# Half of a weight-gradient product moved one step earlier, and the first group's products in another order

## The chip, the cores and the metric

The kernel runs on one core of a Trainium2 chip. A core has a matrix engine (TensorE, PE in the profile, with its weight loads as PEld), a vector engine (VectorE, DVE), a scalar engine (ScalarE, ACT), GpSimd (POOL) and SyncE (SP), which here only issues DMA transfers. Each engine takes its instructions in the order in which they stand in its own queue and waits for the others by semaphores. The metric is the device time of one execution in microseconds, the median of several. Matmul results land in PSUM, a small memory of eight banks, and must be copied out of it (evacuated) by ACT or DVE before the bank can be used again.

## What is computed

It is the backward pass (and the output) of a layer that mixes a spectral filter with a gated feed-forward network, all in bf16, with 2048 rows of 576 and an inner width of 4608:

```python
def _A_ref(x, w_r, w_i):                       # spectral filter
    X = rfft2(x) * (w_r + 1j * w_i)
    return irfft2(X, s=(S, D))

def _B_ref(x, w_gate, w_up, w_down):           # feed-forward
    return (_gelu(x @ w_gate) * (x @ w_up)) @ w_down

g = _sigmoid((x * gate_w).sum(-1, keepdims=True))
out = g * _A_ref(...) + (1 - g) * _B_ref(...)
# results: out, and the gradients for x, w_r, w_i, w_gate, w_up, w_down, gate_w
```

## The kernel before

The kernel has two phases. The first, some 950 us long, goes over the 4608 inner columns in 18 groups (`g` = 0 to 17, `NG`) of 256 columns. Each group is four steps (`m` = 0 to 3, called the first to the fourth step here), and a step takes 512 of the 2048 rows. The code counts steps through as `pr` = 4 g + m. The second phase, from about 980 us to the end, multiplies the stored activations with the weights (L1205) and is not touched.

A step does three kinds of work.

- **The step's own forward part.** `H_mm` (L403) issues the products `z` (grad_out times w_down, L413 and L418) and `xy` (x times w_gate and w_up, L422 and L429, in two halves: `xy_full(0)` and `xy_full(1)`). ACT evacuates them: `H_da` (L441, four instructions) for `z`; `H_act` (L448 the square `q`, L450 `xb`, L451 `hu`) for each half of `xy`. DVE then does `H_ew1` (L456 to L460). `sigs`, that is `H_ew2` (L476 to L491), is issued at the end of the step: sigmoids on ACT and seven or eight elementwise instructions on DVE, which make the tiles `A` and `dH`.
- **Weight gradients of the group before.** `W_units` (L514) makes, for one group, four units `d` (`u_dwd`: d_w_down, L535, 16 matmuls of 288 columns each, in two halves of 8) and four units `w` (`u_dw`: d_w_gate and d_w_up together, L553, 16 matmuls of 512 columns, in quarters of 4) and a `tail` (L567, 32 short matmuls). Each unit ends with an evacuation out of PSUM (L504, on ACT as a rule) and a DMA to the output. Two PSUM buffers (`wps`) take turns among the units. The list that `W_units` returns says which unit goes to which step of the next group: entries 0 to 3 are the four steps, entry 4 is carried over to the first step of the group after that, and the dictionary names what goes inside a step, between `H_da` and `xy_full(0)` (the `tail` in the third step).
- **A spectral unit now and then.** The FFT is cut into small units (two to sixteen matmuls into a PSUM tile `pf`, an evacuation on ACT, sometimes a few instructions on DVE and a DMA). `want(pr)` says how many have to be done by each step. From the ninth step on (`pr` > 7) one of them is put inside `xy_full(1)`. The others are spread between the quarters and halves of the weight units: the loop at L1085 walks through `jobs` (the carried units, then the step's own), adds up their weights (3.45 for a whole `w`, 2.0 for a whole `d`) and issues the next spectral unit when the sum has come to its share. `pf` and `z` share one PSUM buffer (`pz`, `bufs=1`, L350), so a spectral unit waits until the one before it is evacuated, and so does the next step's `z`. Groups 2 to 5 do the forward transforms (L596, L613), groups 6 to 12 the middle part (L705, L794; its products are DVE work that `side_work` issues right after `H_ew1`, L710 to L766), groups 12 to 16 the inverse (L841 to L875).

In every step the order on PE is thus: `z`, the thin part of `xy`, what goes inside, `xy_full(0)`, `xy_full(1)` with a spectral unit in it, and the jobs with the other spectral units between them. ACT and DVE follow in the same order.

One more thing belongs to the opening: `dB` holds grad_out, which the `d` units need scaled by one minus the gate. `scale_dB(k, cp)` (L979) scales the four row tiles 4k to 4k+3, on ACT (L982) or on DVE (L984). Unit `d` reads row tiles 0 to 7 in its first half and 8 to 15 in its second. Steps `pr` = 4 to 7 are those of group 1, which carry group 0's weight units. In `pr` = 6, `run_late` (L1090) puts two loads of function tables and four sines on ACT's queue in front of the first job's evacuation, and for the rest of that step the evacuations of weight units go to DVE instead of ACT (L1091).

Of the kernel before, what the change touches and what calls it, by code (L numbers as in the profile page):

```python
# [255 lines left out]
def kernel(  # L256
# [246 lines left out]
    def wevac(out, in_):  # L503
        wcopy[0](out, in_)  # L504
# [9 lines left out]
    def W_units(g):  # L514
        fsl = slice(g * FG, (g + 1) * FG)
        kt = kept[g]

        def tl(k, t):
            tile_ = kt[t // 4][min(k, 1)]
            return tile_[:, t % 4, :] if k == 0 else tile_[:, t % 4, k - 1, :]  # L520
        dwd_tiles, wp = {}, {}

        def halves(f, us):
            return [(us, lambda: f(0)), (us, lambda: f(1))]

        def wtile(key):
            if key not in wp:
                wp[key] = pw.tile([P, TPB, FG], F32, tag="wps", name="wps")
            return wp[key]

        def u_dwd(fch, h):
            def f(half):
                wps = wtile(("d", fch, h)).rearrange("p a b -> p (a b)")
                for t in range(8 * half, 8 * half + 8):
                    nc.tensor.matmul(wps[:, :288], lhsT=tl(0, t)[:, fch * P:(fch + 1) * P],  # L535
                                     rhs=dB[:, t, h * 288:(h + 1) * 288], start=(t == 0), stop=(t == T - 1))
                if half == 0:
                    return
                if h == 0:
                    dwd_tiles[fch] = stage.tile([P, D], BF16, tag="dwd", name="dwd")  # L540
                dwd = dwd_tiles[fch]
                wevac(dwd[:, h * 288:(h + 1) * 288], wps[:, :288])
                if h == 1:
                    r0 = g * FG + fch * P
                    wst[0].dma_start(out_6[r0:r0 + P, :], dwd[:])
            return halves(f, 1.0)

        def u_dw(c, cuts=(0, 4, 8, 12, T)):

            def f(t0, t1):  # L550
                wps = wtile(("w", c))
                for t in range(t0, t1):
                    nc.tensor.matmul(wps[:].rearrange("p a b -> p (a b)"), lhsT=xn[:, t, c * P:(c + 1) * P],  # L553
                                     rhs=kt[t // 4][1][:, t % 4].rearrange("p k f -> p (k f)"), start=(t == 0), stop=(t == T - 1))
                if t1 < T:
                    return
                dw = dwtile("dw")
                wevac(dw[:], wps[:])
                for k, ov in enumerate((o4v, o5v)):
                    wst[0].dma_start(ov[:, c, fsl], dw[:, k, :])  # L560
            return [(3.45 * (b - a) / T, lambda a=a, b=b: f(a, b)) for a, b in zip(cuts, cuts[1:])]

        def tail():
            wps = wtile("t")
            for t in range(T):
                for k, r in ((1, LO), (2, HI)):
                    nc.tensor.matmul(wps[r, 0, :], lhsT=xn[:, t, 512:576], rhs=tl(k, t),  # L567
                                     start=(t == 0), stop=(t == T - 1))
            dw = dwtile("dwt")
            wevac(dw[:, 0], wps[:, 0, :])  # L570
            wst[0].dma_start(out_4[512:576, fsl], dw[LO, 0, :])
            wst[0].dma_start(out_5[512:576, fsl], dw[HI, 0, :])
        w = [u_dw(c, (0, 12, T)) if g == 0 and c < 2 else u_dw(c) for c in range(4)]
        d = [u_dwd(fch, h) for fch in range(FCH) for h in range(2)]
        if g == 0:
            return [[w[0][:1], w[1][:1]], [d[0], d[1]], [d[2], d[3], w[2][:2]], [w[2][2:], w[3][:3]], w[3][3:], {1: [w[0][1][1], w[1][1][1]], 2: [tail]}]
        return [[d[0]], [d[1], d[2], d[3]], [w[0]], [w[1], w[2]], w[3], {2: [tail]}]


    side = []  # L580
# [305 lines left out]
    VC, AC = V.tensor_copy, nc.scalar.copy  # L886
# [5 lines left out]
    for c in range(6):  # L892
        w = gwr[0:1, eo(c)] if c < 4 else gwr[0:1, 512:D]
# [92 lines left out]
    for g in range(NG):  # L986
# [3 lines left out]
        for m in range(NPR):  # L990
            pr = g * NPR + m
# [9 lines left out]
            tiles = [ewt(tag, g) for tag in ("xb", "q", "hu")]  # L1001
            state = []
# [3 lines left out]
            if g == 0:  # L1006
                def items(src, dst, t, *cp):
                    return titems(src, dst, 4 * t, (pgtile,) * 3, cp) if t < NPR else [None] * 3
                do1 = items(dB, dOT, 1, VC, VC, VC) if m == 0 else []
                do2 = items(dB, dOT, m + 2, AC, AC, VC)  # L1010
                x1 = items(xn, xT, m + 1, AC if m else VC, VC, VC)
                z, xy_full = H_mm(g, m, ([opening] if m == 0 else []) + rest)
                rest = []
                da = H_da(g, m, z)
                if m == 0:
                    early, mid_, late_ = do1[:2], [do1[2], x1[0]], x1[1:]
                elif m < NPR - 1:
                    early, mid_, late_ = x1[:2], x1[2:], []
                else:
                    early, mid_, late_ = [], [], []  # L1020
                for f in early:
                    f()
                xy = xy_full(0)
                for f in mid_:
                    f()
                if held:
                    held.pop()()
                for part in (1, 0):
                    H_act(0, xy, tiles, part)

                def between():
                    for f in late_:
                        f()
                xy = xy_full(1, between)
                for part in range(2):
                    H_act(1, xy, tiles, part)
                if m == 0:
                    build_R(nc, tb, unit, 4)
                    columns_B(nc, tb, res)
                elif m == 1:  # L1040
                    next(makeB)
                if m < NPR - 1:
                    gate(m + 1)
                else:
                    V.tensor_copy(g32[:], g_bf[:])
                    V.tensor_scalar(gs32[:], g32[:], SD2, None, op0=ALU.mult)
                if m + 2 < NPR:
                    do2[0]()
                    do2[1]()
                    rest = [do2[2]]  # L1050
                state += [*H_ew1(g, tiles, da), da]
                held.append(sigs)
            else:
                z, xy_full = H_mm(g, m)
                da = H_da(g, m, z)
                for f in inside:
                    f()
                if pr == 5:
                    scale_dB(2, AC)
                xy = xy_full(0)  # L1060
                if held:
                    scale_dB(0, AC)
                    held.pop()()
                for part in (1, 0):
                    H_act(0, xy, tiles, part)
                k0 = int(n > 0 and pr > 7 and ready())
                xy = xy_full(1, fft_next if k0 else None)
                for part in range(2):
                    H_act(1, xy, tiles, part)
                if pr == 5:  # L1070
                    scale_dB(3, VC)
                state += [*H_ew1(g, tiles, da), da]
                if pr == 4:
                    scale_dB(1, VC)
                elif pr == 5:
                    build_R(nc, tb, unit, 8)
                    build_R(nc, tb, unit, 12)
                elif pr == 6:
                    next(makeB)
                side_work(4.4)  # L1080
                jobs = carry + hs
                total = sum(w for w, _ in jobs)
                at, k = 0.0, k0
                tables = {6: 0}.get(pr)
                for i, (w, f) in enumerate(jobs):  # L1085
                    if k < n and (at >= total * k / n - 0.45 or len(jobs) - i <= n - k):
                        fft_next()
                        k += 1
                    if i == tables:
                        run_late(tb)  # L1090
                        wcopy[0] = VC  # L1091
                    if pr == NG * NPR - 1 and at == 0.0:
                        sigs()
                    f()
                    at += w
                wcopy[0] = AC
                while k < n:
                    fft_next()
                    k += 1
                flush()  # L1100
                if pr == 6:
                    next(makeB)
                if pr < NG * NPR - 1:
                    sigs()
# [250 lines left out]
```

## Time and profile before

| what | us |
|---|---|
| median of 3 executions | 1408.48 (1408.42 to 1409.05) |
| the profiled execution | 1408.48, its span 1406.7 |
| PE busy in the span | 1375.1 |
| DVE busy in the span | 747.7 |
| ACT busy in the span | 713.0 |
| granted TensorE clock | 1.000 |

The span runs from the first to the last instruction; 1.8 us of the execution lie around it. The lengths of single steps, read on PE from one step's first L413 matmul to the next step's:

| stretch (us from the span's start) | what it is | length | PE busy | DVE busy | ACT busy |
|---|---|---|---|---|---|
| 59.00 to 71.94 | group 1, second step | 12.94 | 12.29 | 12.53 | 9.35 |
| 71.94 to 86.89 | group 1, third step | 14.95 | 14.27 | 12.13 | 11.64 |
| 86.89 to 100.26 | group 1, fourth step | 13.37 | 12.63 | 7.93 | 9.72 |
| 713.89 to 728.85 | group 13, third step | 14.96 | 13.62 | 8.57 | 10.52 |
| 728.85 to 743.40 | group 13, fourth step | 14.55 | 14.50 | 9.74 | 9.31 |

A line of the timeline gives start, length, engine, source line, operation, what it writes and reads, the count of merged instructions, and in brackets how long the engine had been idle before it and what ended that. A matmul's length in the trace includes its way through the array: one of 512 columns is shown with 379 ns, though 16 of them in a row take 3.45 us, 0.216 us each (one of 288 columns, L535: 0.1225 us each).

### The profile page before, as it was taken

The numbers are of one execution on the slowest core, as the hardware profiler recorded it, in microseconds if no ns is written. First come the engines' busy times: TensorE is split into PE (matmuls) and PEld (weight loads), VectorE is DVE, ScalarE is ACT, GpSimd is POOL, SyncE is SP. The second block draws the span as 40 slices with busy tenths as digits, with TensorE's granted clock in tenths as the row PEclk, the third lists the DMA queues.
The fourth block names the chain that finished last, engine by engine and source line by source line (L and its number), as shares of the span: only waits on it lengthen the run. The fifth ranks groups of instructions, "written<-read, shape, count | busy, mean of one in ns | idle before, by whom it ended". The sixth has DMA issues, their size and how long they took to land.

```text
span 1406.7 us, 25932 instructions
## 1 busy us (share of the span) xinstructions
PE 1375.1 (98%) x10181; PEld 913.6 (65%) x10272; DVE 747.7 (53%) x1406; ACT 713.0 (51%) x1311; POOL 245.6 (17%) x486
## 2 busy tenths in 40 slices
PE   8999999999999999999999999999999999999999
PEld 6556566565566556556566566555777777777777
DVE  7875655555888778885666666561000642212101
ACT  6877767777778778767777776661000000000000
POOL 3000111023353633423101111110000100000000
DMA  6433435355464655556456464849999998778774
GB/s 214 122 88 109 124 110 133 91 141 159 108 159 131 154 159 155 126 149 164 126 143 173 127 165 132 198 117 278 184 198 196 222 190 168 161 160 163 158 152 89
DMA packets 510646, 214.49 MB, mean 152 GB/s; under 512 B 312538, under 2 KB 503708, under 8 KB 510524
## 3 DMA queue, kind: packets, MB, share of 16 engines
q1 hardware_dynamic: 493402, 187.44, 56.8%
q0 software_dynamic: 14912, 24.24, 6.1%
q8 instruction: 80, 1.31, 0.4%
q10 hardware_dynamic: 2210, 1.15, 0.3%
q14 instruction: 42, 0.34, 0.1%
HBM read 41.05 MB, written 93.84 MB: 96 GB/s over the span
## 4 chain that ended last, share of the span: by engine, by line
PE 55%; ACT 1%; DMA 1%; SPq 1%; DVE 1%; issue 1%; ACTq 0%
PE acc L1205 30%; PE wps L553 7%; PE xy L429 7%; PE wps L535 4%; PE z L413 4%; PE wps L567 1%; DMA wd_all<-in_B_w_down_dram 1%; PE xy L422 1%; SPq L1130 1%; PE z L418 1%; PE pf L867 1%; PE pf L869 1%; ACT ZT L844 0%; PE pf L841 0%; ACT hu L451 0%
## 5 line engine op out<-in xcount | busy, mean ns | idle before, releaser
L1205 PEld LDWEIGHTS <-pin 128*128 128x128 bf16 x3456 | 338.0, 98 | 86.3 <-issue 1.0
L553 PE MATMUL wps<-dH,xn 128*128 128x512 bf16 x1122 | 267.9, 379 | 2.1 <-DVE dwd L504 0.5
L429 PE MATMUL xy<-wgu,xT 128*128 128x512 bf16 x1091 | 258.1, 379 | 8.3 <-issue 7.6
L429 PEld LDWEIGHTS <-xT 128*128 128x128 bf16 x1152 | 106.5, 98 | 133.0 <-issue 24.8
L553 PEld LDWEIGHTS <-xn 128*128 128x128 bf16 x1152 | 111.3, 98 | 118.8 <-issue 1.3
L1222 ACT COPY bo<-acc 128x288 f32<-128x288 f32 x32 | 12.8, 399 | 304.4 <-PE acc L1205 304.4
L535 PE MATMUL wps<-dB,A 128*128 128x288 bf16 x1152 | 154.2, 286 | 0.6 <-DVE dB L984 0.6
L560 POOL DMA_DIRECT2D out_dram<-dw x134 | 72.7, 546 | 441.3 <-ACT dw L504 416.8
L1205 PE MATMUL acc<-wgT,pin 128*128 128x288 bf16 x1152 | 143.9, 286 | 0.3 <-ACT dw L504 0.3
L1205 PE MATMUL acc<-wuT,pin 128*128 128x288 bf16 x1152 | 143.6, 286 | 0.0
L1205 PE MATMUL acc<-wd_all,pin 128*128 128x288 bf16 x1152 | 142.6, 286 | 0.0
L413 PE MATMUL z<-wdT,dOT 128*128 128x256 bf16 x1152 | 137.5, 272 | 2.8 <-ACT Xg L710 1.0
L535 PEld LDWEIGHTS <-A 128*128 128x128 bf16 x1152 | 112.1, 98 | 34.3 <-issue 1.3
L413 PEld LDWEIGHTS <-dOT 128*128 128x128 bf16 x1152 | 112.4, 98 | 26.0 <-issue 5.6
L441 ACT ACTIVATE da<-z,omg 128x256 bf16<-128x256 f32 x288 | 112.1, 471 | 14.9 <-PE z L418 14.1
L450 ACT CAST xb<-xy 128x512 bf16<-128x512 f32 x144 | 85.3, 592 | 48.5 <-PE xy L429 48.5
L1277 DVE SCALAR_TENSOR_TENSOR f32t<-gwf,dlog,b16t 128x576 f32<-128x576 f32 x16 | 13.1, 818 | 173.0 <-DMA b16t<-dxa_scr 173.0
L448 ACT ACTIVATE q<-xy 128x512 bf16<-128x512 f32 x144 | 87.5, 612 | 17.0 <-DVE xb L489 8.6
L483 DVE TENSOR_TENSOR xb<-xb,sg 128x1024 bf16<-128x1024 bf16 x48 | 33.2, 692 | 104.4 <-ACT sg L479 104.4
L451 ACT CAST hu<-xy 128x512 bf16<-128x512 f32 x144 | 87.6, 608 | 0.0
L504 ACT CAST dw<-wps 128x512 bf16<-128x512 f32 x72 | 42.2, 588 | 68.5 <-PE wps L553 56.3
L1236 DVE SCALAR_TENSOR_TENSOR b16t<-b16t,g,f32t 128x576 bf16<-128x576 bf16 x16 | 13.1, 818 | 95.5 <-DMA b16t<-a_scr 95.2
(216 smaller groups left out, 1654.0 us busy)
## 6 DMA issues: line engine op xcount, KB each, us to landing
scr<-dH SPq DMA_DIRECT2D x144, 256.0 KB, 3.4
scr<-A SPq DMA_DIRECT2D x72, 256.0 KB, 2.7
out_dram<-dw POOLq DMA_DIRECT2D x134, 64.0 KB, 2.5
wd_all<-in_B_w_down_dram SPq DMA_DIRECT2D x3, 1728.0 KB, 12.1
out_dram<-dwd POOLq DMA_DIRECT2D x34, 144.0 KB, 3.0
scr_p<-Vt SPq DMA_DIRECT2D x32, 145.0 KB, 2.8
wgu<-in_B_w_gate_dram SPq DMA_DIRECT2D x18, 256.0 KB, 4.1
wgu<-in_B_w_up_dram SPq DMA_DIRECT2D x18, 256.0 KB, 3.6
```

Of the source, the lines that this page charges most:

```text
L413: nc.tensor.matmul(zo(t), lhsT=dOT[:, ci, t, :], rhs=wdT[:, ci, :], start=(t % 4 < 2 and ci == 0), stop=False)
L429: nc.tensor.matmul(xy[k][:, t % 2, :], lhsT=xT[:, ci, t, :], rhs=wgu[:, ci, :], start=False, stop=(ci == 3))
L441: nc.scalar.activation(da[:, t, :], z[:, t % 2, t // 2, :], ACT.Copy, scale=omg32[:, 4 * m + t:4 * m + t + 1])
L448: nc.scalar.activation(q[:, h, :], xy[:, :, 0:FG], ACT.Square)
L450: nc.scalar.copy(xb[:, h, :], xy[:, :, 0:FG])
L451: nc.scalar.copy(hu[:, h, :], xy[:, :, FG:2 * FG])
L483: V.tensor_tensor(xb[:], xb[:], s[:], op=ALU.mult)
L504: wcopy[0](out, in_)
L535: nc.tensor.matmul(wps[:, :288], lhsT=tl(0, t)[:, fch * P:(fch + 1) * P], rhs=dB[:, t, h * 288:(h + 1) * 288], start=(t == 0), stop=(t == ...
L553: nc.tensor.matmul(wps[:].rearrange("p a b -> p (a b)"), lhsT=xn[:, t, c * P:(c + 1) * P], rhs=kt[t // 4][1][:, t % 4].rearrange("p k f -> ...
L560: wst[0].dma_start(ov[:, c, fsl], dw[:, k, :])
L1205: nc.tensor.matmul(acc[:, :288], lhsT=src[:, r, :], rhs=w_of(r)[:, h * 288:(h + 1) * 288], start=(first and r == 0), stop=(last and r == F ...
```

## The change

Two edits, both of the plan alone: the number of instructions on each engine stays the same.

- **Groups 1 to 17** (the second `return` of `W_units`): the third step gets the first two quarters of `w[1]` after `w[0]`, the fourth step begins with the other two quarters.
- **Group 0** (the first `return`, worked off in the steps of group 1): the second step gets all of `w[2]` in place of `d[0]` and `d[1]`; the third step gets all four `d` in place of two `d` and half of `w[2]`; the fourth step gets three quarters of `w[3]` alone. The scaling of `dB` follows: row tiles 4 to 7 on ACT in `pr` = 5, after `H_act` (before: on DVE in `pr` = 4); row tiles 8 to 11 on DVE in `pr` = 5, after `H_ew1` (before: on ACT in `pr` = 5, ahead of `xy_full(0)`); row tiles 12 to 15 on DVE in `pr` = 6, after `H_ew1` (before: on DVE in `pr` = 5, ahead of `H_ew1`).

```diff
         if g == 0:
-            return [[w[0][:1], w[1][:1]], [d[0], d[1]], [d[2], d[3], w[2][:2]], [w[2][2:], w[3][:3]], w[3][3:], {1: [w[0][1][1], w[1][1][1]], 2: [tail]}]
-        return [[d[0]], [d[1], d[2], d[3]], [w[0]], [w[1], w[2]], w[3], {2: [tail]}]
+            return [[w[0][:1], w[1][:1]], [w[2]], [d[0], d[1], d[2], d[3]], [w[3][:3]], w[3][3:], {1: [w[0][1][1], w[1][1][1]], 2: [tail]}]
+        return [[d[0]], [d[1], d[2], d[3]], [w[0], w[1][:2]], [w[1][2:], w[2]], w[3], {2: [tail]}]
...
                 for f in inside:
                     f()
-                if pr == 5:
-                    scale_dB(2, AC)
                 xy = xy_full(0)
...
                 for part in range(2):
                     H_act(1, xy, tiles, part)
+                state += [*H_ew1(g, tiles, da), da]
                 if pr == 5:
-                    scale_dB(3, VC)
-                state += [*H_ew1(g, tiles, da), da]
-                if pr == 4:
-                    scale_dB(1, VC)
-                elif pr == 5:
+                    scale_dB(1, AC)
+                    scale_dB(2, VC)
                     build_R(nc, tb, unit, 8)
                     build_R(nc, tb, unit, 12)
                 elif pr == 6:
+                    scale_dB(3, VC)
                     next(makeB)
```

## The prediction

> **What bounds the kernel now.** I read the page's first part, then the lengths of single steps, then the timeline of PE, ACT and DVE through some of them.
>
> ```profile
> PE 1375.1 (98%) x10181; PEld 913.6 (65%) x10272; DVE 747.7 (53%) x1406; ACT 713.0 (51%) x1311; POOL 245.6 (17%) x486
> ```
>
> PE is the bound, and the change alters no instruction, only the order, so only PE's idle time can be won or lost. The busy time hides some of it, because a matmul's shown length overlaps the gap behind it. I therefore measure a step by its length. The next lines are the busy times by stretch (length, PE, PEld, DVE, ACT, POOL, clock, DMA): third and fourth step of group 16, which have no spectral unit, and of group 6.
>
> ```profile
> 879.32:890.70 11.38, 11.22 (x90) 6.60 (x88) 6.72 (x11) 7.38 (x14) 1.61 (x3) 1.00 0.98 211
> 890.70:903.67 12.97, 12.81 (x73) 6.49 (x72) 7.06 (x12) 6.92 (x13) 2.18 (x4) 1.00 0.87 223
> ...
> 349.30:363.17 13.87, 12.44 (x95) 7.17 (x94) 8.60 (x15) 11.10 (x21) 5.18 (x11) 1.00 0.42 111
> 363.17:376.63 13.46, 13.25 (x74) 6.88 (x76) 11.83 (x24) 8.90 (x16) 2.18 (x4) 1.00 0.14 41
> ```
>
> A third step needs 11.38 us of PE, a fourth 12.97, and a spectral unit of two matmuls 0.245 (two of 0.1225). Group 6's third step has three units: 11.38 + 0.73 = 12.11, but lasts 13.87, so 1.75 are lost. Its fourth has two: 12.97 + 0.49 = 13.46, nothing lost. Done for groups 2 to 15 (other units at 0.74 for six matmuls, 0.44 for eight of 128 columns, 0.50 for six of the inverse), the third steps lose 0.47, 0.72, 1.10, 1.68, 1.75, 0.84, 0.69, 1.75, 0.01, 0, 0.02, 1.55, 0.43, 0.70: 11.7 us. The fourth lose 2.3 (1.11 in group 8, 0.88 in group 10), the second 2.2. First steps, which have 5.41 us of jobs, lose 1.3 over groups 3 to 15.
>
> PE's timeline shows where group 6 loses it, between the quarters of `w[0]`; ACT's shows why.
>
> ```profile
> 357.48 1.03 PE L553 MATMUL wps<-dH,xn 128*128 128x512 bf16 x4
> 358.49 0.41 PE L705 MATMUL pf<-Vp,Btab 128*128 128x289 bf16 x2
> 358.74 1.89 PE L553 MATMUL wps<-dH,xn 128*128 128x512 bf16 x8
> 361.39 0.41 PE L705 MATMUL pf<-Vp,Btab 128*128 128x289 bf16 x2 [0.76 <-ACT Xx L710]
> 361.63 1.02 PE L553 MATMUL wps<-dH,xn 128*128 128x512 bf16 x4
> 363.17 1.91 PE L413 MATMUL z<-wdT,dOT 128*128 128x256 bf16 x16 [0.51 <-ACT Xg L710]
> ```
>
> ```profile
> 359.42 0.61 ACT L451 CAST hu<-xy 128x512 bf16<-128x512 f32 x1
> 360.05 1.28 ACT L710 CAST Xx<-pf 64x578 bf16<-64x578 f32 x2
> 361.83 1.29 ACT L710 CAST Xg<-pf 64x578 bf16<-64x578 f32 x2 [0.49 <-PE pf L705]
> ```
>
> The second unit is evacuated only after ACT has finished `hu`; the third unit and the next `z` need the same PSUM buffer and wait. The jobs between the units (3.45 us) are too short to cover evacuations of 1.3 us.
>
> **Part one: half of `w[1]` into the third step.** Eight matmuls of 0.216 move, 1.73 us; jobs become 5.18 us in both steps. Nothing else of the unit moves: its evacuation (0.58 on ACT) and two DMA issues on POOL stay in the fourth step; SP's queue is passed by nothing. By the loop's rule the spectral units of group 6 now stand inside `xy` and after 8 and 16 of 24 matmuls, instead of after 4 and 12 of 16.
>
> Group 9's third step, laid out from its rows: `xy` ends 514.41; eight matmuls to 516.14; second unit; its evacuation 516.96 to 518.25 as before; eight to 518.1; third unit at 518.31 (0.2 lost); evacuated 520.04; eight to 520.3. It ended at 520.09, so 0.2 is added for 1.73 moved in. The fourth step sheds the whole 1.73 (units at 528.1 and 530.1, evacuations in time): 1.5 won.
>
> Group 6 is the other kind. Its third and fourth steps win 1.55 likewise, but there DVE and ACT run in a loop of their own: `H_ew1`, spectral products, `H_ew2` up to L489, then ACT's `q`, which waits for it. Two of these waits, and what PE pays:
>
> ```profile
> 382.54 0.60 ACT L448 ACTIVATE q<-xy 128x512 bf16<-128x512 f32 x1 [0.30 <-DVE s L489]
> 394.86 0.60 ACT L448 ACTIVATE q<-xy 128x512 bf16<-128x512 f32 x1 [0.39 <-DVE s L489]
> ...
> 399.87 0.41 PE L705 MATMUL pf<-Vp,Btab 128*128 128x289 bf16 x2 [0.38 <-ACT Xx L710]
> ```
>
> DVE is busy without a pause longer than 0.4 from 372.1 to 396.3, so these instants stay where they are. PE, 1.55 earlier, waits 0.7 at its second unit of group 7's first step and 1.0 at 399.87: all given back by 402.08. In the same way groups 10 and 11 win 0: group 10's 0.85 is lost at 595.43, and group 11's third step, which loses nothing now, becomes 1.73 longer while the fourth waits for `q` at 629.92. Groups 7 and 8 keep 0.75 and 0.8.
>
> In groups 2 to 5 and 13 to 15 DVE is 8 to 10 us busy per step and not in the way. With units between one or two quarters, the layout gives 0.4, 0.65, 0.7, 0.8 and 0.85, 0.4, 0.5; group 12 has nothing to win. Sum: 4.3 there + 0.75 + 0.8 + 1.5 = 7.35. I take off 0.6 for fourth steps that now have 5.18 us of jobs for four or five units (0.1 for each of six, the first steps' 1.3 over thirteen being the nearest row). Part one: -6.75. Bounds: +4.6 to -10; the first is priced as the slower rival, the second is the 11.7 less those 1.3 and a little.
>
> **Part two: the first group's products.** Before, the second step of group 1 stalled on `dB`:
>
> ```profile
> 69.02 3.08 PE L535 MATMUL wps<-dB,A 128*128 128x288 bf16 x20 [0.60 <-DVE dB L984]
> ...
> 85.17 1.89 PE L553 MATMUL wps<-dH,xn 128*128 128x512 bf16 x7 [0.47 <-DVE dwd L504]
> ```
>
> Second step: 32 matmuls of 0.1225 (3.92) give way to 16 of 0.216 (3.46), and the stall goes (1.2 with the matmuls that follow at the scaling's pace of 0.3): it ends at 66.79 + 3.46 = 70.25 instead of 71.94. ACT is rid of 2.81 us (L982) ahead of `xb` and has them after `hu`, behind which only `w[2]`'s evacuation and a sigmoid stand; both are ready in time. On POOL's queue the two transfers of `w[2]` now go ahead of the first `d`'s; only the staging tiles wait for them, and `w[2]` takes the one that `w[0]` filled some 6 us before (a transfer lands in 2.5).
>
> Third step: `xy` ends 1.69 earlier, at 78.18. `H_ew1` runs from about 79.0 to 81.1 (it follows `xy`'s end by 0.8), then the last scaling, 1.20 for four. PE reaches row tile 12 at 78.18 + 0.74 + 12 x 0.1225 = 80.4 and waits until 81.45; the last four go at DVE's 0.3. The first `d` ends at 82.4, the second at 84.4. DVE makes the table instructions (82.78 to 84.7 before, now to 84.1) and only then evacuates the first `d`, so the third starts at 84.6 and the fourth ends at 88.5, 1.6 later than before. Who queues behind the scaling is these evacuations, and PE waits for them. `H_ew2` follows at 89.1; ACT's sigmoid for it is ready at 87.2, after two table loads of 1.28 each (82.20 and 86.47 before) and four sines of 2.56.
>
> Fourth step: jobs 2.59 instead of 4.32, with the same four units, each of which waits for the evacuation of the last: 0.9 lost behind `hu`, then 0.85 in front of the next `z`. It ends at 100.9 instead of 100.26. Part two: +0.7. Bounds: -1.0 (without the third step's 1.7 of waits) to +3.5 (the second and third `d` also wait 1.3 each for evacuations behind DVE's tables).
>
> The row for a table load is 1.28, and the next activation starts 0.02 later (82.20, 83.50). The Trainium skill, "ScalarE: Activation LUTs", section "What ACT_TABLE_LOAD costs", adds a drain of about 1.38 us to each load. The trace shows no drain; by that rule the sigmoid would come at about 90.0, `H_ew2` 0.9 later, and part two would be +1.6.
>
> **Sum.** -6.75 + 0.7 = -6.05 on the profiled 1408.48 (span 1406.7 and 1.8 around it), which is the median itself: 1402.4. The second phase starts as much earlier, because the loads in front of it wait for the last group's stores.
>
> **Rivals.**
> *The DVE loop takes more (0.21).* If in the groups with products (6 to 11) all is given back, and the inverse's third steps keep half of their idle time, 2.55 + 0.9 = 3.4 are won, less 0.7: 1405.8; with the forward ones halved too, 1407. For it: DVE is 12 to 14 us busy in those steps as counted with overlaps, against a fourth step of 11.98 (12.97 + 0.73 - 1.73). Against: pauses of 1.5 to 4 us on DVE in groups 9 to 12.
> *Slower (0.17).* The shortened fourth step falls under the DVE-ACT loop. Place: fourth steps of groups 6 to 11. Price: busy DVE 13.6 less 11.98 is 1.6 in each, 9.7, against 5.0 that the third steps of these groups lose today: +4.7. With 0.7 of part two and nothing won elsewhere, 1413.9; with half of that, 1411. It decides if the lag cannot slide into the next first step (12.22 long, DVE 10 to 12.5 busy) and the third steps stay bound by ACT's evacuations.
> *All the idle time goes (0.06).* -10 + 0.7: 1399. For it the first steps; against it group 6.
> That the change is not carried out is excluded: the order of the built instructions shows the eight matmuls moved in each group.
>
> **How the numbers follow.** My forecast has 0.56 with its own range 1399.5 to 1405.5. About 0.2% (2.8 us) is what a measurement tells from no change: below 1405.7 is faster, above 1411.3 slower. Faster: 0.56 + 0.06, less a little, plus a part of the first rival: 0.61. Same: most of the first rival and the slower one's mild half: 0.22. Slower: 0.17. The range of eight in ten is 1398.5 to 1411.0, from the rival with all idle time won to the mild half of the slower one.
>
> **What will show it.** Third steps longer by 0.2 to 1.1, fourth steps of groups 2 to 5, 9, 13 to 15 shorter by 1.6 to 1.73; the waits for Xg, Xx, ZT and ve before the third steps' ends gone; group 7's first two steps longer by 1.5 together; the wait on `dB` at 69.02 gone and one of about 1 us in the third step of group 1, and group 2 starting near 100.9. Wrong would be: fourth steps that do not shrink, third steps that grow by the full 1.73, or a third step of group 1 beyond 20 us.

## The result, and the profile after

| | before | after |
|---|---|---|
| median (range) | 1408.45 us (1408.11 to 1409.05, 6 runs) | 1403.21 us (1403.08 to 1404.81, 6 runs) |
| profiled execution, its span | 1408.48, 1406.7 | 1403.11, 1401.2 |

The ratio of after to before is 0.9964, with a 95% interval of 0.9951 to 0.9977: faster by 0.36%. The forecast was 1402.4.

First the busy times of the whole span in the profile of after:

```profile
PE 1373.5 (98%) x10187; PEld 913.6 (65%) x10272; DVE 748.9 (53%) x1408; ACT 710.7 (51%) x1309; POOL 245.1 (17%) x486
```

PE's busy time went down by 1.6 us while the span went down by 5.5. The rest was idle time, so this line alone can't say where it came from. The lengths of single steps can. The next lines are the busy times by stretch of after (length, PE, PEld, DVE, ACT, POOL, clock, DMA): third and fourth step of group 6, and of group 16, which has no spectral unit in them.

```profile
347.80:361.85 14.05, 13.85 (x103) 7.96 (x102) 8.77 (x16) 11.76 (x22) 6.27 (x13) 1.00 0.41 110
361.85:373.59 11.74, 11.58 (x68) 6.09 (x68) 10.18 (x21) 8.05 (x15) 1.08 (x3) 1.00 0.06 19
...
874.30:887.41 13.11, 12.95 (x98) 7.35 (x96) 6.72 (x11) 8.91 (x16) 2.26 (x5) 1.00 0.96 219
887.41:898.65 11.24, 11.08 (x64) 5.72 (x64) 7.15 (x12) 5.31 (x12) 1.53 (x3) 1.00 0.86 211
```

Group 16 shows the move alone: its third step went from 11.38 to 13.11, its fourth from 12.97 to 11.24, both by 1.73. Group 6 shows the gain: its third step took in the same eight matmuls and grew by 0.19 only, since 13.11 + 3 x 0.245 = 13.85 is now needed and 14.05 is used. Its fourth shed 1.72. PE's timeline of after shows the third step's jobs without a wait:

```profile
355.97 1.89 PE L553 MATMUL wps<-dH,xn 128*128 128x512 bf16 x8
357.70 0.41 PE L705 MATMUL pf<-Vp,Btab 128*128 128x289 bf16 x2
357.95 1.89 PE L553 MATMUL wps<-dH,xn 128*128 128x512 bf16 x8
359.88 0.41 PE L705 MATMUL pf<-Vp,Btab 128*128 128x289 bf16 x2
360.13 1.89 PE L553 MATMUL wps<-dH,xn 128*128 128x512 bf16 x8
361.85 0.82 PE L413 MATMUL z<-wdT,dOT 128*128 128x256 bf16 x6
```

Eight matmuls (1.73 us) stand behind every spectral unit. Both waits that stood here before, 0.76 for Xx and 0.51 for Xg, are gone.

Summed over the lengths of steps, the time went like this: opening -0.22, group 1 +0.73, groups 2 to 17 -5.53, second phase -0.5. Together -5.5, the difference of the two spans. By kind of step in groups 2 to 17: the third ones +19.09, the fourth -26.66, the first +1.30, the second +0.74.

### The profile page after: what moved, and what is told of

Read it like the earlier page. It is cut to its first block, busy times and chain, and to the rows that moved or that the text cites. A ratio compares the mean times of both kernels' runs of the same rounds, so it can differ in the third digit from the quotient of the medians.

```text
span 1401.2 us, 25933 instructions
## 1 busy us (share of the span) xinstructions
PE 1373.5 (98%) x10187; PEld 913.6 (65%) x10272; DVE 748.9 (53%) x1408; ACT 710.7 (51%) x1309; POOL 245.1 (17%) x486
## 3 DMA queue, kind: packets, MB, share of 16 engines
q8 instruction: 80, 1.31, 0.4%
## 4 chain that ended last, share of the span: by engine, by line
PE 56%; DVE 1%; ACT 1%; issue 0%; DMA 0%; SPq 0%; DVEq 0%; ACTq 0%
PE acc L1202 30%; PE wps L553 7%; PE xy L429 6%; PE wps L535 4%; PE z L413 3%; PE wps L567 1%; PE xy L422 1%; PE z L418 1%; PE pf L867 1%; PE pf L869 1%; ACT ZT L844 0%; PE pf L841 0%; ACT q L448 0%; DMA wdT<-wdT 0%; ACT Xg L710 0%
## 5 line engine op out<-in xcount | busy, mean ns | idle before, releaser
L456 DVE TENSOR_SCALAR s<-q 128x1024 bf16<-128x1024 bf16 x72 | 30.7, 426 | 67.1 <-ACT q L448 67.1
```

## The experiments

All runs of one batch share their runs of the kernel before. Besides the times I give the change in step lengths against the profile of before ("by steps"). That measure repeats to 0.05 us a step from run to run, while the time of an execution also moves with short falls of PE's granted clock, which the last section shows.

**The two parts apart.** The first kernel has only the moved quarters, the second only the first group's new order (the change with the second `return` put back).

```diff
-        return [[d[0]], [d[1], d[2], d[3]], [w[0]], [w[1], w[2]], w[3], {2: [tail]}]
+        return [[d[0]], [d[1], d[2], d[3]], [w[0], w[1][:2]], [w[1][2:], w[2]], w[3], {2: [tail]}]
```

> Part one alone: two quarters of w[1] in the third step of groups 1 to 17, the first group's order as before the change. My theory: the whole gain is here and the first group's new order costs 0.7 (its group 2 starts 0.51 + 0.22 later in the trace of the changed kernel), so this one is faster than the changed kernel: 1402.5, with the third and fourth steps of groups 2 to 17 as long as there. Rival (the gain comes from the first group, where the wait on dB went): about 1408.

> Part two alone: the first group's units and scaling as in the changed kernel, third and fourth steps of groups 1 to 17 as before. My theory: 1408.45 + 0.7 = 1409.2, second step of group 1 1.70 shorter, third 3.3 longer, fourth 0.9 shorter, all later steps of the same length as before. Rival (it helps, and the two parts add): below 1408.

Measured: the quarters alone 1402.36 (1402.24 to 1402.89) against 1408.75 before, ratio 0.9951, interval 0.9938 to 0.9965; by steps -5.49 in groups 2 to 17. The first group alone 1409.38 (1409.08 to 1410.96), ratio 1.0004, interval 0.9995 to 1.0012: no difference by its time, but +0.73 by steps in group 1. All of the gain is in the first edit, and the second takes a little away.

**How many quarters.** The same line with one, three and all four quarters of `w[1]` in the third step.

```diff
-[w[0]], [w[1], w[2]]
+[w[0], w[1][:1]], [w[1][1:], w[2]]
...
+[w[0], w[1][:3]], [w[1][3:], w[2]]
...
+[w[0], w[1]], [w[2]]
```

> One quarter of w[1] moved instead of two, first group's order as before the change. My theory (idle time of the third steps goes as jobs between the spectral units grow): jobs of 4.31 and 6.04, about half of the third steps' 11.7 of idle time goes and nothing comes back in the fourth steps: 1405 (1404 to 1406.5). Rival (each quarter counts in full until the DVE loop takes it): the same as two quarters, 1402.5 to 1403.

> Three quarters of w[1] moved, first group's order as before the change: jobs of 6.04 and 4.31. My theory: fourth steps begin to lose as third steps did, third steps are clear; in groups 6 to 11 the DVE loop holds the fourth steps: 1403 to 1406, worse than two quarters by 1 to 3. Rival (the fourth step, which has less on ACT, takes it): 1400 to 1402.

> All of w[1] moved: jobs of 6.9 in the third step and 3.45 in the fourth, first group's order as before the change. My theory: the idle time changes places. The third steps lose nothing, the fourth steps as much as the third did (11.7 in sum), and in groups 6 to 11, where the fourth step needs 10.3 of PE and the DVE loop takes 12 to 13, more: slower than two quarters by 6 to 15, 1409 to 1418. Rival (PE's idle time in the third step comes from its tail and ACT's sigmoid, not from the length of the jobs): the fourth step takes it without idle time, 1400 to 1403.

| quarters moved | median us | ratio (95%) | groups 2-17 by steps | of it 2-5 | 6-11 | 12-15 |
|---|---|---|---|---|---|---|
| one | 1405.80 | 0.9978 (0.9969 to 0.9987) | -2.53 | -1.00 | -1.61 | +0.07 |
| two | 1402.36 | 0.9951 (0.9938 to 0.9965) | -5.49 | -2.00 | -2.49 | -0.99 |
| three | 1408.49 | 1.0001 (0.9992 to 1.0010) | +0.48 | -0.70 | -1.12 | +1.87 |
| four | 1415.24 | 1.0042 (1.0030 to 1.0055) | +8.09 | -1.69 | +8.28 | +1.50 |

The times with one and with four quarters came as expected. Three did not: they lose all of the gain. In groups 12 to 15 the fourth steps, relieved of 4 x 2.59 = 10.4 us of matmuls, became only 6.05 shorter. The waits of PE for ACT over groups 12 to 15 (what waits, for what, us in total, times, longest), with three quarters:

```profile
PE pf L853 <- ACT ev L873: 1.4, 2, 0.7
PE pf L867 <- ACT ZT L844: 1.1, 2, 0.9
PE pf L867 <- ACT ZU L856: 0.6, 1, 0.6
PE z L413 <- ACT ZT L844: 0.2, 1, 0.2
```

and in the changed kernel:

```profile
PE pf L867 <- ACT ZT L844: 0.6, 2, 0.4
PE z L413 <- ACT ZT L844: 0.2, 1, 0.2
PE pf L853 <- ACT ev L873: 0.2, 1, 0.2
```

They add up to 3.3 against 1.0. The idle time has moved from the third step into the fourth: five quarters (4.3 us) are now too few for its four or five units, as four quarters were in the third step. With all four moved something else comes up, in group 8, which loses 5.56 of the 8.28. ACT, DVE and PE of that kernel:

```profile
474.00 0.59 ACT L504 CAST dw<-wps 128x512 bf16<-128x512 f32 x1 [5.08 <-DMA out_dram<-dwt]
```

```profile
475.58 0.69 DVE L483 TENSOR_TENSOR xb<-xb,s 128x1024 bf16<-128x1024 bf16 x1 [4.86 <-ACT s L476]
```

```profile
477.06 0.41 PE L705 MATMUL pf<-Vp,Btab 128*128 128x289 bf16 x2 [1.67 <-ACT da L441]
...
481.43 0.41 PE L705 MATMUL pf<-Vp,Btab 128*128 128x289 bf16 x2 [2.23 <-ACT Xx L710]
```

The evacuation of the whole `w[1]` at the third step's end waits for the transfer of the `tail`'s output, as the profile infers from the semaphores. ACT's sigmoid stands behind it, DVE behind the sigmoid, `q` behind DVE and PE behind `q`. No evacuation waits for that transfer in the kernel before or after. Not all of the 5.56 is due to it: in this profile the granted clock is 0.50 for 3.41 us from 482.25 on, in the fourth step of this group, which costs some 1.7 us if PE's work there is taken as half done (an estimate).

**Is it the DVE loop that takes group 6's gain back?** First by leaving DVE work out: the products `o` and their combination (L730 at 0.76 each and L740 at 0.83 for two, 2.35 of DVE a time), so that the gradients of w_r and w_i are not computed; in the kernel before, and with two quarters moved.

```diff
-                o = st[p, "o1"]
+                o = G
...
-                (0.8, mul("o1", G, X[:, :, 0, :])), (0.8, mul("o2", G, X[:, :, 1, :])), (0.85, comb("o1", "o2", True)),
```

> The kernel before with three of the fourteen spectral product instructions groups left out on DVE (o1, o2 and their combination, 2.4 us for each of the eight blocks; the gradients of w_r and w_i are not computed, their place is filled with other data by the same transfers). It shows what the DVE loop costs before the change. Expected: third steps of groups 6 to 9 idle as before (they wait for ACT), the idle time of second and fourth steps in groups 7 to 10 (about 3.1) mostly gone: 1405.5 (1404.5 to 1407).

> The same left out, and two quarters of w[1] moved in groups 1 to 17 (first group's order as before the change). My theory: what group 6 won was given back to the DVE loop (1.5), and group 10 won only 0.3; with the loop relieved they keep it, so the move is worth 1.5 to 3 more than without: 7 to 8.5 less than the same kernel without the move. Rival (it was given back for another reason, ACT's own load or PSUM): the move is worth the same 5.5 to 6.

Measured: 1407.51 (1406.55 to 1409.73) without `o`, ratio 0.9995 (0.9986 to 1.0004), where 1405.5 was expected; 1400.84 (1400.58 to 1402.07) with the quarters as well, ratio 0.9945 (0.9933 to 0.9958). The move is thus worth 6.7 by medians, less than expected, and by steps (-7.24 against -1.63) 5.61, hardly more than the 5.49 with `o` in place. Group 7's first step is longer by 1.00 even here. DVE's timeline tells why: at 376.30 the next product, `m`, stands where `o` had been, because the loop fills its allowance with whatever comes next. So this pair did not take the suspected work out of the suspected place, and tells nothing for or against the loop. What it told of the second phase stands below.

The next pair does it. The allowance is lowered by a hair, which pushes one product out of the stretch between `H_ew1` and `H_ew2` of group 6's fourth step.

```diff
-                side_work(4.4)
+                side_work(4.3)
```

> The run with two quarters moved and the first group as before (1402.36), with one more thing: the allowance for spectral products after H_ew1 is 4.3 instead of 4.4 in the loop's count, which takes one product (L730 into o, 0.76 us) out of the fourth step of group 6 and puts it, and two of the half-combinations after it, a step later. Nothing is left out. If the DVE loop is what takes group 6's 1.5 back in group 7, then H_ew2 and ACT's q come 0.76 earlier there, the first step of group 7 is longer than before by 0.2 to 0.3 instead of 0.96, its second by 0 to 0.6 instead of 0.59, and the time is 1401.0 to 1401.8. If it is ACT's evacuations alone, the two steps stay as they are and the time is 1402.4.

> The kernel before with the same allowance of 4.3. If the DVE loop binds only where a step has become shorter, PE had in this kernel just 0.4 us to win at the second step of group 7 and about as much in group 8: 1407.5 to 1408.5, which a measurement hardly tells from no change. If the loop binds everywhere in groups 6 to 11, each of its steps gains and the time is 1406 or less.

ACT's timeline in group 7 with the quarters alone, and then with the shorter stretch as well:

```profile
380.96 0.60 ACT L448 ACTIVATE q<-xy 128x512 bf16<-128x512 f32 x1 [1.85 <-DVE s L489]
...
393.27 0.60 ACT L448 ACTIVATE q<-xy 128x512 bf16<-128x512 f32 x1 [0.97 <-DVE s L489]
```

```profile
379.71 0.60 ACT L448 ACTIVATE q<-xy 128x512 bf16<-128x512 f32 x1 [1.17 <-DVE s L489]
...
391.75 0.60 ACT L448 ACTIVATE q<-xy 128x512 bf16<-128x512 f32 x1 [0.72 <-DVE s L489]
```

ACT waits 0.68 less for DVE, and group 7's first step is longer than before by 0.27 instead of 0.96, its second by 0.33 instead of 0.59, both in the expected ranges. Groups 8 and 11 gain too (0.76 and 0.35). By steps the kernel stands at -7.47 instead of -5.49. Its median of 1402.63, ratio 0.9951 (0.9939 to 0.9963), is above the expected range and does not show that: the two executions with a mean granted clock of 1.000 took 1400.89 and 1400.91, the three with 0.999 took 1402.63 to 1404.65. So it is the steps that show the loop, not the median.

In the kernel before the same edit gave 1408.45 (1407.26 to 1409.53) against 1409.08, ratio 0.9995 (0.9986 to 1.0004), in the expected range. By steps, though, it won 1.31, more than the 0.8 expected: 0.49 in the second step of group 7 and 0.86 in group 8, and the second phase took back 1.03 of it. At these places PE thus waits for the loop before the change as well. What the loop takes back only from shortened steps is the rest: 0.69 in group 7's first step and 0.35 in group 11's, where the kernel before gains nothing by this edit. Of the 1.55 that group 7's first two steps lose with the quarters alone, 0.95 goes away with the shorter stretch; what holds the other 0.60 was not separated.

**Group 14's fourth step.** The third and fourth spectral unit between its jobs one quarter earlier, so that the last is followed by two quarters.

```diff
-                    if k < n and (at >= total * k / n - 0.45 or len(jobs) - i <= n - k):
+                    if k < n and (at >= total * k / n - (0.7 if pr == 59 else 0.45) or len(jobs) - i <= n - k):
```

> The run with two quarters moved and the first group as before (1402.36); in the fourth step of group 14 alone the third and the fourth spectral unit between the jobs stand one quarter earlier, so that the last one is followed by two quarters instead of one. If that one quarter was why this step became shorter by 1.01 only, z's wait of 0.24 is gone and the step is 1.4 to 1.7 shorter than before: 1401.8 to 1402.0. If it is the other units, it stays at 1.0 and the time at 1402.4.

PE at the end of that step, after and then with the edit:

```profile
792.27 0.61 PE L841 MATMUL pf<-RT,Vp 128*128 128x128 bf16 x8
792.72 1.03 PE L553 MATMUL wps<-dH,xn 128*128 128x512 bf16 x4
793.98 1.91 PE L413 MATMUL z<-wdT,dOT 128*128 128x256 bf16 x16 [0.24 <-ACT ZT L844]
```

```profile
791.25 0.61 PE L841 MATMUL pf<-RT,Vp 128*128 128x128 bf16 x8
791.69 1.89 PE L553 MATMUL wps<-dH,xn 128*128 128x512 bf16 x8
793.42 1.91 PE L413 MATMUL z<-wdT,dOT 128*128 128x256 bf16 x16
```

The evacuation of the last unit takes 1.01, a quarter covers 0.86. With two quarters behind it the wait of 0.24 is gone and the step is 1.41 shorter than before instead of 1.01. The time, 1402.45 (1401.91 to 1403.44), ratio 0.9952 (0.9940 to 0.9965), cannot tell 0.4. Some 0.3 stay open in that step; a wait of 0.19 for `ev` in its middle is part of it.

**Both together.**

> Both of these together: the gains add up, since they lie in groups 7 and 14: 1400.5 to 1401.4. If only one of the two holds, the time is that of the one.

Measured: 1400.75 (1400.22 to 1401.57) against 1409.08, ratio 0.9939, interval 0.9925 to 0.9953; by steps -7.91. It has the lowest median and the lowest ratio of all the kernels here, as expected from two gains that lie in different groups.

**The scaling ahead of `H_ew1`.** The changed kernel, with the last scaling of `dB` before `H_ew1` in step 6 instead of behind it.

```diff
+                if pr == 6:
+                    scale_dB(3, VC)
                 state += [*H_ew1(g, tiles, da), da]
...
-                    scale_dB(3, VC)
```

> The changed kernel with the last scaling of dB (row tiles 12 to 15) ahead of H_ew1 instead of after it, in the same step. My theory: the wait of 0.94 on dB goes, but the first unit's evacuation stays behind the table instructions on DVE (83.86 in the changed kernel), so the third unit waits there instead: same time within 0.3. Rival (the wait on dB is the price of the new order): 1.2 to 1.5 faster, 1401.8.

Measured: 1404.16 (1402.74 to 1404.34), ratio 0.9965 (0.9953 to 0.9977). By steps group 1's third step is 0.49 shorter than in the changed kernel, a little more than expected. The median cannot show it: five of the six executions had a mean granted clock of 0.999 and took 1404.01 to 1404.34; the one with 1.000 took 1402.74, against 1403.08 to 1403.41 of the changed kernel at 1.000. PE's rows there:

```profile
80.42 4.08 PE L535 MATMUL wps<-dB,A 128*128 128x288 bf16 x32
85.60 4.08 PE L535 MATMUL wps<-dB,A 128*128 128x288 bf16 x32 [1.10 <-DVE dwd L504]
```

The wait on `dB` is gone, and 1.10 for the evacuations of the first `d` units takes its place, because DVE still makes the tables before it evacuates. That is the wait the prediction named as next, and it decides.

## Why the prediction was right, and where its sizes were off

**The mechanism** held. Idle time between the quarters of third steps was the price of evacuations of 1.3 us between jobs that were too short, and eight more matmuls covered them.

**Part one** was forecast at -6.75 and is -5.53 by steps. Groups 2, 3, 4, 9, 13 and 15 gave 0.39, 0.52, 0.66, 1.53, 0.78 and 0.59, each within 0.13 of the layout; group 12 gave nothing, as said. Groups 6 and 7 gave 0.82 together: 1.53 won in group 6, taken back in group 7's first two steps (1.54), and 0.82 won in its third and fourth, where 0.75 was said. ACT's `q` in group 7 stands at 381.04 instead of 382.54; that is the 1.5 which all the steps ahead of group 6 had won, so group 6's own 1.53 did not move it, as forecast. PE's waits are where they were put, 0.60 and 0.83 against 0.7 and 1.0 forecast. ACT, then PE:

```profile
381.04 0.60 ACT L448 ACTIVATE q<-xy 128x512 bf16<-128x512 f32 x1 [1.84 <-DVE s L489]
```

```profile
382.39 0.41 PE L794 MATMUL pf<-qn,BTtab 128*128 128x290 bf16 x2 [0.60 <-ACT Vt L797]
...
398.37 0.41 PE L705 MATMUL pf<-Vp,Btab 128*128 128x289 bf16 x2 [0.83 <-ACT Xx L710]
```

Groups 10 and 11 together lost 0.07 where 0 was said, but not by the path that was said: group 10's fourth step won 0.30, not 0.85, group 11's first step took back 0.37, and its fourth step shed the whole 1.73, where the prediction had it wait for `q`. Three terms were mis-sized. Group 14 lost 0.33 instead of winning 0.4: by the loop's rule the last unit of its shortened fourth step got one quarter behind it, which the layout had not placed; by the experiment above this makes 0.40 of the 0.72 that the step fell short, and the rest is open. Group 8 won 0.24 instead of 0.8: its third step grew by 1.10, where the forecast allows 0.93, its fourth step has a wait of 1.11 and shrank by 1.48 only, and its second step grew by 0.14.

```profile
477.02 0.41 PE L705 MATMUL pf<-Vp,Btab 128*128 128x289 bf16 x2 [1.11 <-ACT Xg L710]
```

Group 5 won 0.46 instead of 0.8, all of it missing in its third step (+1.26): one quarter still stands between its last two units, and PE's wait there, 0.51 for `RT`, is as long as before. The allowance of 0.6 was meant for fourth steps with four or five units. These fell short of 1.73 by 0.72 in group 14, 0.13 in group 4 and 0.03 or 0.04 in groups 2, 3, 12 and 15: 1.0 together, most of it in one step.

**Part two** was forecast at +0.7 and is +0.73 (second step -1.70, third +3.31, fourth -0.88). PE's timeline of after through group 1:

```profile
78.69 1.63 PE L535 MATMUL wps<-dB,A 128*128 128x288 bf16 x12
81.27 7.18 PE L535 MATMUL wps<-dB,A 128*128 128x288 bf16 x52 [0.94 <-DVE dB L984]
88.28 1.91 PE L413 MATMUL z<-wdT,dOT 128*128 128x256 bf16 x16
...
100.77 1.47 PE L413 MATMUL z<-wdT,dOT 128*128 128x256 bf16 x12 [0.79 <-ACT ve L616]
```

In a run whose opening is 0.22 shorter, the wait on `dB` is 0.94 and ends at 81.27 (81.45 forecast), at row tile 12 as laid out; the fourth `d` ends at 88.28 (88.5); `z` of group 2 waits 0.79 for `ve` (0.85) and stands at 100.77 (100.9). ACT's rows for the two table loads:

```profile
80.28 1.28 ACT L177 ACT_TABLE_LOAD   x1
81.57 2.56 ACT L177 ACTIVATE Rt<-XR,pi 128x512 bf16<-128x512 int32 x4
...
84.55 1.28 ACT L476 ACT_TABLE_LOAD   x1
85.84 1.06 ACT L476 ACTIVATE s<-s 128x1024 bf16<-128x1024 bf16 x1
```

The next activation starts 0.01 after each load of 1.28 (0.02 before), and the sigmoid is done 2.3 before DVE wants it at 89.19. The Trainium skill's page "ScalarE: Activation LUTs", section "What ACT_TABLE_LOAD costs", would have put a drain of about 1.38 us on top of each; the rows show none.

**The second phase** was forecast to start as much earlier as the groups end; it came 0.5 better. The rows around its start in the kernel before: ACT, the chain of work that ended last, and PE.

```profile
975.97 3.83 ACTq L560 DMA_DIRECT2D out_dram<-dw  x2
979.84 0.58 ACT L504 CAST dw<-wps 128x512 bf16<-128x512 f32 x1 [3.90 <-DMA wd_all<-in_B_w_down_dram]
```

```profile
966.93 12.50 DMA wd_all<-in_B_w_down_dram
979.44 0.02 issue
979.46 0.34 ACTq L560
```

```profile
978.52 1.63 PE L1205 MATMUL acc<-wgT,pin 128*128 128x288 bf16 x12
980.47 7.51 PE L1205 MATMUL acc<-wgT,pin 128*128 128x288 bf16 x60 [0.32 <-ACT dw L504]
```

PE in the kernel before without `o`, and ACT in the changed kernel:

```profile
980.17 7.51 PE L1204 MATMUL acc<-wgT,pin 128*128 128x288 bf16 x60 [1.76 <-ACT dw L504]
```

```profile
970.87 0.85 ACTq L560 DMA_DIRECT2D out_dram<-dw  x2
973.71 0.59 ACT L504 CAST dw<-wps 128x512 bf16<-128x512 f32 x1 [2.87 <-PE wps L553]
976.86 1.13 ACTq L560 DMA_DIRECT2D out_dram<-dw  x2
```

In the kernel before, ACT's last evacuation stands behind two issues of output transfers. The row of 3.83 holds both: each takes 0.34, and the second one waits until 979.44, when the second of three loads of wd_all, issued at 966.93, has landed. In the trace this load and that output transfer count on one semaphore (number 100). A group phase that is 1.75 shorter, as in the kernel without `o`, reaches this floor only earlier: PE's wait grows from 0.32 to 1.76. After the change the second load counts on another semaphore (102), which the very last output transfer uses too; that one waits until 976.86, and no evacuation stands behind it. The last evacuation is at 973.71, and PE does not wait. The other kernels agree: the four with the old plan of groups 1 to 17 have semaphore 100 at this load, and PE waits (0.32, 0.4 with the first group's order alone, 1.76, and 1.23 with the shorter loop); all those with one to four quarters moved have another one, and PE doesn't wait. With three quarters an earlier pair of issues on ACT is held for 5.30 by the first load, but the last evacuation is done at 980.16, just in time for a first phase that ends at 978.82. So the 0.5 comes from which transfers share a semaphore; why the moved quarters change that was not followed up.

**The number** owes something to luck. On the profiled executions -6.05 was forecast and -5.50 measured. The groups gave only -4.80; 0.48 of the second phase and 0.22 of a shorter opening, neither of them forecast, made up for over half of what was missing.

**The rivals.** "All is given back in groups 6 to 11" fell: these groups kept 2.52. "The shortened fourth step falls under the loop" fell too: their fourth steps shrank by 10.40, all of 6 x 1.73, and what slid into first and second steps was 2.04. Something like it came with four quarters, where these groups lose 8.28; but 5.56 of this lies in group 8, where a transfer and a fall of the clock have a part in it.

## What to carry to other kernels

Where small units with one PSUM buffer are strewn between long accumulations, the work behind each unit, the last one above all, must be longer than its evacuation and what stands ahead of it on that engine; move work into the short stretch until the donor is about to become the short one, and no further (two quarters won 5.5, three nothing, four cost 8, some 1.7 of it by the clock). Measure an engine by start-to-start lengths against a stretch without the suspect: a busy share of 98% did not show that third steps alone lose 11.7 us here. Before counting a gain, look at what the next phase waits for: a load that shares a semaphore with an output transfer was a floor just 0.3 below. Before trusting a median, look at the granted clock of each execution.

## What the runs showed of the hardware

PE's granted clock can fall to half in the middle of a run. In the profiled executions with one quarter and with the scaling first it is 0.50 for 3.41 us, from 14.95 and from 15.14 on, and the very first step took 1.66 to 1.68 longer than the 14.44 of the others, about half of 3.41. With four quarters such a fall of 3.41 us comes at 482.25. The busy times by stretch around the first fall, with the scaling first and then after the change, where the clock stays at 1.00:

```profile
15.20:18.50 3.30, 3.30 (x14) 1.50 (x12) 2.07 (x5) 1.76 (x5) 0.00 (x0) 0.50 1.02 393
...
15.10:18.40 3.30, 3.25 (x30) 2.02 (x29) 2.98 (x7) 2.88 (x9) 0.00 (x0) 1.00 1.02 385
```

PE is shown as busy in both, with 14 matmuls in one and 30 in the other. 1.7 us is as much as single experiments here were to tell. What sets the fall off is open: PE's wait of 0.97 just ahead of it stands in the kernel before as well, without a fall.

The issue of an output transfer on ACT took 0.46 and 0.34 in the kernel before (at 974.86 and 979.46), but it can be held by another queue's transfer that counts on the same semaphore: 3.83 (before) and 4.01 (without `o`) for a pair of issues, the second of which waited for a load of 1728 KB that SP had issued. The evacuation behind it on ACT waits as long.
